# A streamed x + alpha * fx on one core: loads and stores interleaved, against all loads first and all stores last

## The chip, the core and the metric

The kernel runs on one core of a Trainium2 chip. The metric is the time of one execution on the device in microseconds (us); the median of three runs stands for a kernel. Beside it one profiled execution gives the trace that is read here. Its span goes from the first to the last instruction on the core and is a little shorter than the time of a run.

## What is computed

```python
B, S, D = 512, 32, 640
x, fx: bfloat16 [512, 32, 640]      # 20.97 MB each
alpha: bfloat16 [1]

def reference(x, fx, alpha):
    return x + alpha * fx
```

Two arrays are read, one of the same size is written, and each element is used once: 62.92 MB pass through the core.

## The kernel before

x, fx and out are seen as 128 partitions with one row each of 81,920 elements, which is 160 KiB in bf16. `K = 1024` elements, 2 KiB, is the unit in which the lists `X` and `FX` cut the row. x comes in three chunks (of 64, 64 and 32 KiB per partition) into a pool `wide` of two buffers; fx comes in five chunks (32, 32, 38, 32 and 26 KiB) into a pool `fs` of two buffers. `X_CUTS` splits the first chunk of x into transfers of 8 and 56 KiB, and `F_CUTS` splits the third of fx into 32 and 6 KiB.

`PLAN` is the order of the program, written out by hand, and it is all there is of loops: `x i` loads a chunk of x (`load_x`, L87), `f j` one of fx (`load_f`, L96), `a` loads alpha (L133) and spreads it over 128 partitions by a matmul of a row of ones (L135, L137) and a copy out of PSUM (L139), `c j i` computes where chunk j of fx and chunk i of x overlap (`compute`, L108), and `s i` stores a chunk (`store`, L121).

All transfers are issued by SyncE (SP) on one queue, in the order of the plan. SP waits, at an issue, for what that transfer needs, and everything behind it waits too. The computation is one instruction of VectorE for each piece, `scalar_tensor_tensor`, that multiplies fx by alpha and adds x in one pass, and writes over x. A store thus waits for the passes over its chunk. A load waits until the buffer is free: the third chunk of x for the end of the first store, later chunks of fx for the passes that read the earlier ones. One wait more is set by hand (`AFTER`): the first store is not issued before the first 32 KiB of the third chunk of fx have landed; the other 6 KiB are then still under way.

At the end SP waits for all transfers (a `nop`, L148).

Of the kernel before, what the change touches and what calls it, by code (L numbers as in the profile page):

```python
# [2 lines left out]

# [4 lines left out]

ACT = mybir.ActivationFunctionType
ALU = mybir.AluOpType  # L10
F32 = mybir.dt.float32
BF16 = mybir.dt.bfloat16

K = 1024
P = 128


X = [(0, 32), (32, 64), (64, 80)]
FX = [(0, 16), (16, 32), (32, 51), (51, 67), (67, 80)]

F_CUTS = {2: (48,)}
S_CUTS = {}
AFTER = {("s", 0): ("f", 2, 48)}
X_CUTS = {0: (4,)}
PLAN = """
x 0
a
f 0
f 1
x 1  # L30
c 0 0
f 2
c 1 0
s 0
f 3
x 2
c 2 1
f 4
c 3 1
c 3 2  # L40
s 1
c 4 2
s 2
"""


@with_exitstack
def kernel(
    ctx: ExitStack,
    tc: tile.TileContext,  # L50
    x: bass.AP,
    fx: bass.AP,
    alpha: bass.AP,
    out: bass.AP,
):

    nc = tc.nc
    xv = x.flatten_outer_dims().rearrange("(p n) d -> p (n d)", p=P)
    fxv = fx.flatten_outer_dims().rearrange("(p n) d -> p (n d)", p=P)
    ov = out.flatten_outer_dims().rearrange("(p n) d -> p (n d)", p=P)
    assert xv.shape[1] == X[-1][1] * K == FX[-1][1] * K

    consts = ctx.enter_context(tc.tile_pool(name="consts", bufs=1))
    psum = ctx.enter_context(tc.tile_pool(name="psum", bufs=1, space=bass.MemoryType.PSUM))
    wide = ctx.enter_context(tc.tile_pool(name="wide", bufs=2))
    fs = ctx.enter_context(tc.tile_pool(name="fs", bufs=2))  # L70
    ctx.enter_context(tc.manual_schedule())

    parts = {}
    info = mybir.DependencyInfo(mybir.DependencyClass.Sync, mybir.DependencyReason.DATA)

    def after(r, *what):
        if what in AFTER:
            tc.add_manual_dep(r.ins, parts[AFTER[what]].ins.name, info, reason="issue late")

    xt, ft = {}, {}  # L80
    done = []

    def load_x(i):
        a, b = X[i]
        xt[i] = wide.tile([P, max(e - s for s, e in X) * K], x.dtype, tag="x", name="x_t")
        for c, d in pairwise((a, *X_CUTS.get(i, ()), b)):
            r = nc.sync.dma_start(  # L87
                out=xt[i][:, (c - a) * K : (d - a) * K], in_=xv[:, c * K : d * K]
            )
            done.append(r)  # L90

    def load_f(j):
        a, b = FX[j]
        ft[j] = fs.tile([P, max(e - s for s, e in FX) * K], fx.dtype, tag="f", name="f_t")
        for c, d in pairwise((a, *F_CUTS.get(j, ()), b)):
            r = nc.sync.dma_start(  # L96
                out=ft[j][:, (c - a) * K : (d - a) * K],
                in_=fxv[:, c * K : d * K],
            )
            after(r, "f", j)  # L100
            done.append(r)
            parts["f", j, d] = r

    def compute(j, i):
        (fa, fb), (xa, xb) = FX[j], X[i]
        a, b = max(fa, xa), min(fb, xb)
        piece = xt[i][:, (a - xa) * K : (b - xa) * K]
        r = nc.vector.scalar_tensor_tensor(  # L108
            out=piece,
            in0=ft[j][:, (a - fa) * K : (b - fa) * K],  # L110
            scalar=lanes["a_f"][:],
            in1=piece,
            op0=ALU.mult,
            op1=ALU.add,
        )
        done.append(r)

    def store(i):
        a, b = X[i]
        for c, d in pairwise((a, *S_CUTS.get(i, ()), b)):  # L120
            r = nc.sync.dma_start(  # L121
                out=ov[:, c * K : d * K], in_=xt[i][:, (c - a) * K : (d - a) * K]
            )
            if c == a:
                after(r, "s", i)
            done.append(r)
            parts["s", i, d] = r

    lanes = {}

    def alpha_to_lanes():
        a_1 = consts.tile([1, 1], alpha.dtype, name="a_1")
        done.append(nc.sync.dma_start(out=a_1[:], in_=alpha[None, :]))  # L133
        ones = consts.tile([1, P], alpha.dtype, name="ones")
        nc.vector.memset(ones[:], 1.0)  # L135
        a_ps = psum.tile([P, 1], F32, name="a_ps")
        done.append(nc.tensor.matmul(a_ps[:], ones[:], a_1[:], start=True, stop=True))  # L137
        lanes["a_f"] = consts.tile([P, 1], F32, name="a_f")
        nc.vector.tensor_copy(out=lanes["a_f"][:], in_=a_ps[:])  # L139

    does = {"x": load_x, "f": load_f, "c": compute, "s": store, "a": alpha_to_lanes}
    for step in PLAN.split("\n"):
        if step:
            what, *of = step.split()
            does[what](*map(int, of))


    rest = nc.sync.nop(nofuse=True)  # L148
    for i in done[:-1]:
        tc.add_manual_dep(rest.ins, i.ins.name, info, reason="all but the last store")  # L150


# [1 line left out]
_INS = ['x', 'fx', 'alpha']  # L154
_OUTS = [((512, 32, 640), 'bfloat16')]


# [23 lines left out]
```

## Time and profile before

| | |
|---|---|
| median of 3 runs | 151.9 us (151.71 to 151.95) |
| span of the profiled execution (no other time is given for it) | 150.2 us |
| bytes read, written | 41.94 MB, 20.97 MB |
| mean rate over the span | 419 GB/s |

The page has a row for each engine (busy time and share of the span), for the DMA queue (packets, megabytes, share of the time of 16 DMA engines), and for groups of instructions: line, engine, operation, names and shapes, then busy time and mean duration, then the idle time before them and what ended it. Lines of the timeline and of the chain of waits begin with the start and the duration in us; SPq is SyncE issuing a transfer. Issue rows give the size and the time from issue to landing. A row of the view by windows has the stretch, its length, the busy time of four compute engines, the granted clock, the DMA share and GB/s; there a packet counts where it starts, so a window must be laid on the packets to be read.

### The profile page before, as it was taken

To read this page: it belongs to the slowest core of one execution; us is meant where nothing else is said; L and a number is where in the kernel's file an instruction comes from. 1 tells how busy PE (TensorE), PEld (TensorE's weight loads), DVE (VectorE), ACT (ScalarE), POOL (GpSimd) and SP (SyncE) were. 2 spreads that over 40 slices of the span, in tenths; PEclk is the share of its full clock that TensorE was granted. 3 is DMA by queue.
4 is the path that set the end of the run, shared out by engine and by line. 5 is a ranking of instruction groups with operands and counts; after the bars stand their busy time and mean duration, and the time that the engine had idled before them with its cause. 6 is when DMAs were issued, how large, how long until landed. Compare 5 with 4: busy or idle time off the path is not lost.

```text
span 150.2 us, 81 instructions
## 1 busy us (share of the span) xinstructions
PE 0.2 (0%) x1; PEld 0.1 (0%) x1; DVE 86.8 (58%) x8; POOL 0.2 (0%) x4
## 2 busy tenths in 40 slices
PE   0000000000000000000000000000000000000000
PEld 0000000000000000000000000000000000000000
DVE  0000000049999999970599998006999999980000
POOL 0000000000000000000000000000000000000000
DMA  5997999999999896999969696999999969697995
GB/s 179 589 412 321 489 384 419 419 445 436 515 419 489 349 559 279 419 419 397 650 279 559 279 559 279 419 419 419 428 469 418 570 279 559 279 559 314 428 436 218
DMA packets 1874, 62.92 MB, mean 419 GB/s; under 512 B 210, under 2 KB 210, under 8 KB 338
## 3 DMA queue, kind: packets, MB, share of 16 engines
q1 hardware_dynamic: 1874, 62.92, 98.1%
HBM read 41.94 MB, written 20.97 MB: 419 GB/s over the span
## 4 chain that ended last, share of the span: by engine, by line
DMA 53%; DVE 35%; SPq 1%; issue 0%; DVEq 0%
DMA f_t<-in_fx_dram 53%; DVE x_t L108 35%; SPq L87 1%; SPq L96 0%; SPq L133 0%; DVEq L108 0%
## 5 line engine op out<-in xcount | busy, mean ns | idle before, releaser
L108 DVE SCALAR_TENSOR_TENSOR x_t<-f_t,a_f,x_t 128x16384 bf16<-128x16384 bf16 (+3 forms) x6 | 86.5, 14438 | 25.5 <-DMA f_t<-in_fx_dram 25.5
L139 DVE COPY a_f<-a_ps 128x1 f32<-128x1 f32 x1 | 0.2, 157 | 21.4 <-PE a_ps L137 21.4
L135 DVE MEMSET ones<- 1x128 bf16 x1 | 0.2, 165 | 0.8 <-PEq L165 0.8
L137 PE MATMUL a_ps<-a,ones 1*128 1x1 bf16 x1 | 0.2, 159 | 22.2 <-DMA a<-in_alpha_dram 22.2
L165 POOL MEMSET const-bfloat16-1.0<- 128x1 bf16 x1 | 0.1, 103 | 0.0
L165 POOL MEMSET const-uint8-127<- 128x1 uint8 x1 | 0.1, 102 | 0.0
L137 PEld LDWEIGHTS <-ones 1*128 1x128 bf16 x1 | 0.1, 100 | 1.0 <-DVE ones L135 1.0
L165 POOL MEMSET const-float32-0.0<- 128x1 f32 x1 | 0.1, 100 | 0.2 <-issue 0.2
L165 POOL MEMSET const-float32-1.0<- 128x1 f32 x1 | 0.1, 99 | 0.0
## 6 DMA issues: line engine op xcount, KB each, us to landing
f_t<-in_fx_dram SPq DMA_DIRECT2D x4, 4096.0 KB, 30.6
x_t<-in_x_dram SPq DMA_DIRECT2D x1, 7168.0 KB, 21.2
x_t<-in_x_dram SPq DMA_DIRECT2D x1, 4096.0 KB
out_dram<-x_t SPq DMA_DIRECT2D x1, 4096.0 KB, 14.9
f_t<-in_fx_dram SPq DMA_DIRECT2D x1, 3328.0 KB, 26.9
x_t<-in_x_dram SPq DMA_DIRECT2D x1, 1024.0 KB, 4.6
f_t<-in_fx_dram SPq DMA_DIRECT2D x1, 768.0 KB, 23.0
out_dram<-x_t SPq DMA_DIRECT2D x2, 22.4
```

Source lines behind the costliest of these rows:

```text
L87: r = nc.sync.dma_start(out=xt[i][:, (c - a) * K : (d - a) * K], in_=xv[:, c * K : d * K])
L108: r = nc.vector.scalar_tensor_tensor(out=piece, in0=ft[j][:, (a - fa) * K : (b - fa) * K], scalar=lanes["a_f"][:], in1=piece, op0=ALU.mult ...
L135: nc.vector.memset(ones[:], 1.0)
L137: done.append(nc.tensor.matmul(a_ps[:], ones[:], a_1[:], start=True, stop=True))
L139: nc.vector.tensor_copy(out=lanes["a_f"][:], in_=a_ps[:])
L165: nc = _bacc.Bacc("TRN2", target_bir_lowering=False, num_devices=1)
```

## The change

The kernel's body is written anew. The unit `K` is now 512 elements, 1 KiB per partition. One flat tile `t` of 207.5 KiB per partition holds everything: x and the result lie at their own places, 0 to 160, and pieces of fx lie where there is room: beyond 160, and at places of x that is not loaded yet. `f a b p` loads fx from a to b to the place p; `place` finds it again.

The order: x from 0 to 64 (as 8 and 56 KiB), fx 0-64 (into the place of x 96-160), x 64-96, fx 64-111.5 (beyond 160). From there each load is issued when the passes over what lies in its place are done: x 96-114 after the add to 18, x 114-155 after the add to 64, fx 111.5-137.5 after the add to 88, fx 137.5-160 after the add to 111.5, x 155-160 after the add to 113.5. Only then come the stores, of 64, 64 and 32 KiB. The step `s 0 64 | f 137.5 160 184` carries a wait set by hand: the first store is issued when the last piece of fx has landed, and the 5 KiB of x 155-160 are the only load behind that piece on the queue.

The fused pass is replaced by two: `m`, `tensor_scalar_mul` of fx by alpha in place, rounded to bf16, and `c`, `tensor_add` of that to x in place. Alpha is loaded to eight partitions instead of one, right behind the first 8 KiB of x; the matmul reads one of them.

```diff
-K = 1024
 P = 128
+K = 512
+ROW = 160
+SPARE = 47.5
+
+LANES = 8
...
 PLAN = """
-x 0
+x 0 8
 a
-f 0
-f 1
-x 1
-c 0 0
-f 2
-c 1 0
-s 0
-f 3
-x 2
-c 2 1
-f 4
-c 3 1
-c 3 2
-s 1
-c 4 2
-s 2
+x 8 64
+f 0 64 96
+x 64 96
+f 64 111.5 160
+m 0 18
+c 0 18
+x 96 114
+m 18 64
+c 18 64
+x 114 155
+m 64 88
+c 64 88
+f 111.5 137.5 158
+m 88 111.5
+c 88 111.5
+f 137.5 160 184
+m 111.5 113.5
+c 111.5 113.5
+x 155 160
+s 0 64 | f 137.5 160 184
+m 113.5 137.5
+c 113.5 137.5
+m 137.5 160
+c 137.5 160
+s 64 128
+s 128 160
 """
...
-    wide = ctx.enter_context(tc.tile_pool(name="wide", bufs=2))
-    fs = ctx.enter_context(tc.tile_pool(name="fs", bufs=2))
+    flat = ctx.enter_context(tc.tile_pool(name="flat", bufs=1))
...
+    t = flat.tile([P, int((ROW + SPARE) * K)], x.dtype, name="t")
...
+    def place(a, b):
+        for c, d, p in reversed(lies):
+            if c <= a and b <= d:
+                return at(p + a - c, p + b - c)
...
+    def load_f(a, b, p):
+        lies.append((a, b, p))
+        done.append(nc.sync.dma_start(out=at(p, p + b - a), in_=of(fv, a, b)))
...
+        a_n = consts.tile([LANES, 1], alpha.dtype, name="a_n")
+        done.append(nc.sync.dma_start(out=a_n[:], in_=alpha[None, :].to_broadcast([LANES, 1])))
...
-        r = nc.vector.scalar_tensor_tensor(
-            out=piece,
-            in0=ft[j][:, (a - fa) * K : (b - fa) * K],
-            scalar=lanes["a_f"][:],
-            in1=piece,
-            op0=ALU.mult,
-            op1=ALU.add,
-        )
+    def multiply(a, b):
+        done.append(nc.vector.tensor_scalar_mul(place(a, b), place(a, b), lanes["a"][:]))
+
+    def add(a, b):
+        done.append(nc.vector.tensor_add(at(a, b), at(a, b), place(a, b)))
...
+        for other in later:
+            tc.add_manual_dep(done[-1].ins, begun[other].ins.name, info, reason="begins late")
```

More of the change, by code (lines that the diff above doesn't have):

```diff
@@ L1 @@
 from contextlib import ExitStack
-from itertools import pairwise
 import concourse.bass as bass
@@ L7 @@
 from concourse._compat import with_exitstack
-ACT = mybir.ActivationFunctionType
 ALU = mybir.AluOpType
 F32 = mybir.dt.float32
-BF16 = mybir.dt.bfloat16
-K = 1024
 P = 128
[L18 to L24, printed above, removed]
+K = 512
+ROW = 160
+SPARE = 47.5
+LANES = 8
 PLAN = """
-x 0
+x 0 8
 a
-f 0
-f 1
-x 1
-c 0 0
-f 2
-c 1 0
-s 0
-f 3
-x 2
-c 2 1
-f 4
-c 3 1
-c 3 2
-s 1
-c 4 2
-s 2
+x 8 64
[24 more added lines that the diff above has]
+s 128 160
 """
@@ L61 @@
     nc = tc.nc
[L62 to L65, printed above, removed]
+    xv, fv, ov = (
+        t.flatten_outer_dims().rearrange("(p n) d -> p (n d)", p=P) for t in (x, fx, out)
+    )
+    assert xv.shape[1] == ROW * K
     consts = ctx.enter_context(tc.tile_pool(name="consts", bufs=1))
@@ L68 @@
     psum = ctx.enter_context(tc.tile_pool(name="psum", bufs=1, space=bass.MemoryType.PSUM))
-    wide = ctx.enter_context(tc.tile_pool(name="wide", bufs=2))
-    fs = ctx.enter_context(tc.tile_pool(name="fs", bufs=2))
+    flat = ctx.enter_context(tc.tile_pool(name="flat", bufs=1))
     ctx.enter_context(tc.manual_schedule())
-    parts = {}
+    t = flat.tile([P, int((ROW + SPARE) * K)], x.dtype, name="t")
     info = mybir.DependencyInfo(mybir.DependencyClass.Sync, mybir.DependencyReason.DATA)
-    def after(r, *what):
-        if what in AFTER:
-            tc.add_manual_dep(r.ins, parts[AFTER[what]].ins.name, info, reason="issue late")
@@ L80 @@
-    xt, ft = {}, {}
+    lanes = {}
+    lies = []
     done = []
[L83 to L88, printed above, removed]
-            )
[L90 to L108, printed above, removed]
-            out=piece,
-            in0=ft[j][:, (a - fa) * K : (b - fa) * K],
-            scalar=lanes["a_f"][:],
-            in1=piece,
-            op0=ALU.mult,
-            op1=ALU.add,
[L115 to L133, printed above, removed]
+    def at(a, b):
+        return t[:, int(a * K) : int(b * K)]
+    def of(v, a, b):
+        return v[:, int(a * K) : int(b * K)]
+    def place(a, b):
+        for c, d, p in reversed(lies):
+            if c <= a and b <= d:
+                return at(p + a - c, p + b - c)
+        raise ValueError(f"fx {a} to {b} lies nowhere in one piece")
@@ L136, in alpha_to_lanes, with store @@
         a_ps = psum.tile([P, 1], F32, name="a_ps")
[L137 to L145, printed above, removed]
+        done.append(nc.tensor.matmul(a_ps[:], ones[:], a_n[0:1, :], start=True, stop=True))
+        lanes["a"] = consts.tile([P, 1], F32, name="a_f")
+        nc.vector.tensor_copy(out=lanes["a"][:], in_=a_ps[:])
+    def multiply(a, b):
+        done.append(nc.vector.tensor_scalar_mul(place(a, b), place(a, b), lanes["a"][:]))
+    def add(a, b):
+        done.append(nc.vector.tensor_add(at(a, b), at(a, b), place(a, b)))
+    def store(a, b):
+        done.append(nc.sync.dma_start(out=of(ov, a, b), in_=at(a, b)))
+    does = {"x": load_x, "f": load_f, "a": load_alpha, "m": multiply, "c": add, "s": store}
+    begun = {}
+    for step in filter(None, PLAN.split("\n")):
+        step, *later = step.split(" | ")
+        what, *numbers = step.split()
+        does[what](*map(float, numbers))
+        begun[step] = done[-1]
+        for other in later:
+            tc.add_manual_dep(done[-1].ins, begun[other].ins.name, info, reason="begins late")
     rest = nc.sync.nop(nofuse=True)
```

3 lines of the change are left out of this document (added).

## The prediction

> **What bounds the kernel now.** I read the page's totals first, to see which resource is full.
>
> ```profile
> span 150.2 us, 81 instructions
> PE 0.2 (0%) x1; PEld 0.1 (0%) x1; DVE 86.8 (58%) x8; POOL 0.2 (0%) x4
> q1 hardware_dynamic: 1874, 62.92, 98.1%
> ```
>
> One queue moves 62.92 MB, and its packets fill the 16 DMA engines for 98.1% of the span; VectorE works 58% of it. The DMA queue is the bound. A gain can only come out of what it loses now, and a loss comes from anything that leaves it empty.
>
> Next the chain of waits, the issues and the times to landing, to cut the span into stages of the queue. Sizes are in KiB per partition (1 KiB is 128 KiB in all, 512 elements); 480 of them pass, 320 in and 160 out.
>
> ```profile
> 0.73 0.38 SPq L87
> 1.16 0.42 SPq L87
> 1.99 30.13 DMA f_t<-in_fx_dram
> 49.92 22.95 DMA f_t<-in_fx_dram
> 93.51 26.93 DMA f_t<-in_fx_dram
> ```
> ```profile
> 2.96 0.45 SPq L87 DMA_DIRECT2D x_t<-in_x_dram  x1
> 71.09 0.35 SPq L121 DMA_DIRECT2D out_dram<-x_t  x1
> 71.48 0.43 SPq L96 DMA_DIRECT2D f_t<-in_fx_dram  x1
> 92.87 0.33 SPq L87 DMA_DIRECT2D x_t<-in_x_dram  x1
> 102.61 17.41 DVE L108 SCALAR_TENSOR_TENSOR x_t<-f_t,a_f,x_t 128x13312 bf16<-128x13312 bf16 x2 [9.13 <-DMA f_t<-in_fx_dram]
> 116.72 0.34 SPq L121 DMA_DIRECT2D out_dram<-x_t  x1
> 134.58 0.34 SPq L121 DMA_DIRECT2D out_dram<-x_t  x1
> ```
> ```profile
> x_t<-in_x_dram SPq DMA_DIRECT2D x1, 7168.0 KB, 21.2
> out_dram<-x_t SPq DMA_DIRECT2D x1, 4096.0 KB, 14.9
> x_t<-in_x_dram SPq DMA_DIRECT2D x1, 1024.0 KB, 4.6
> x_t<-in_x_dram SPq DMA_DIRECT2D x1, 58.3
> ```
>
> Landings follow: the first 8 KiB of x at 0.73 + 4.6 = 5.33; x to 64 at 1.16 + 21.2 = 22.36; f to 32 at 1.99 + 30.13 = 32.12; x from 64 to 128 at 2.96 + 58.3 = 61.26; f to 96 at 71.09, when the first store is issued on it; f to 102 at 72.87; store 0 at 92.87, when the load that needs its buffer is issued; f to 134 at 102.61; f to 160 at 120.44; the last store at 134.58 + 14.9 = 149.48. Time per KiB: 0.3041 for the 56 KiB of x, 0.3035 for the 96 KiB from 32.12 to 61.26, **0.3125 for store 0** (20.0 us for 64), 0.3044 for the load after it, **0.3074 for the 58 KiB that end at 120.44**, 0.3025 for the last 96 KiB, all stores. Loads alone and stores alone run alike; two stages at a change of direction run slower. Windows laid on the packets there:
>
> ```profile
> 70.30:72.30 2.00, 0.00 (x0) 0.00 (x0) 0.00 (x0) 0.00 (x0) 1.00 1.59 676
> 72.30:74.70 2.40, 0.00 (x0) 0.00 (x0) 1.70 (x1) 0.00 (x0) 1.00 1.01 437
> 86.50:88.90 2.40, 0.00 (x0) 0.00 (x0) 2.40 (x1) 0.00 (x0) 1.00 1.01 437
> 88.90:91.70 2.80, 0.00 (x0) 0.00 (x0) 2.80 (x1) 0.00 (x0) 1.00 1.05 374
> 117.20:119.60 2.40, 0.00 (x0) 0.00 (x0) 2.40 (x1) 0.00 (x0) 1.00 1.17 437
> ```
>
> The last two columns are the DMA share and GB/s; a window counts the packets that start in it. The byte rate over the share is the rate of a busy engine set: 437/1.01 = 433 GB/s in mid-stage. In 88.90 to 91.70, the last piece of store 0 with a load queued behind it, it is 374/1.05 = 356: 1.05 MB were busy for 2.94 us instead of 2.42, **0.52 us lost**. In 117.20 to 119.60, the last piece of f with store 1 behind it, 437/1.17 = 374: 2.81 instead of 2.42, **0.39 lost**. In 70.30 to 72.30, before store 0, 676/1.59 = 425: 3.18 instead of 3.12, 0.06 lost. The engines are busy in all three: these are slow packets, not an empty queue.
>
> **The change part by part.** *Order of the queue.* Bytes stay at 480 KiB per partition; 6 + 4 + 3 large transfers replace 4 + 6 + 3, so nothing is added there, and the first 8 KiB and the last 32 KiB are as before. Three changes of direction become one. Removed: the store-to-load one (0.52) and one of the load-to-store ones. The one left is issued when f has landed, with 5 KiB of x behind it, 5 x 0.3035 = 1.52 us. Its price lies between 0.06 and 0.39; I take 0.06, since its nearest row is store 0, issued 1.78 us ahead of the end of what was queued (71.09 to 72.87), and not store 1, issued some 3 us ahead. By this count the gain is 0.52 + 0.39 + 0.06 - 0.06 = 0.91. By stages: 5.33 + 312 x 0.3035 = 100.0 for the loads, + 160 x 0.3025 = 48.4 for the stores, + 0.06 = 148.5 against 149.48, a gain of 1.0; with all loads at 0.3041 to 0.3044, as three of the stages ran, 0.2 to 0.3 less. I take **0.8 us**, with 0.5 (only the store-to-load price goes) and 1.0 as its ends.
>
> *The start of the first store.* Does 1.52 us of cover suffice? The lead from issue to data: the first load is issued at 0.73, and
>
> ```profile
> 1.00:1.50 0.50, 0.00 (x0) 0.10 (x1) 0.00 (x0) 0.00 (x0) 1.00 0.00 0
> 1.50:2.00 0.50, 0.00 (x0) 0.00 (x0) 0.00 (x0) 0.00 (x0) 1.00 0.88 197
> ```
>
> so data start 0.8 to 1.3 later. With some 0.1 from landing to issue the store's data come at most 1.4 after the landing: covered, by 0.1 at least. If the cover did not count at all, 1.4 would be lost. The Trainium skill (DMA: Bandwidth & Descriptors, Anatomy of one DMA) gives a transfer a fixed cost near 2.0 us, most of it the receipt of the last byte, stated for another path of issue. By that the store would come about 0.5 late, for a time near 151.6; store 0 here, issued on a landing, followed without a gap after at most 1.78 us, so the trace puts the sum below 1.8 and cannot say more.
>
> *VectorE.* Each fused pass becomes a multiply in place and an add. Their rows:
>
> ```profile
> L108 DVE SCALAR_TENSOR_TENSOR x_t<-f_t,a_f,x_t 128x16384 bf16<-128x16384 bf16 x2 | 34.5, 17281 | 9.7 <-DMA f_t<-in_fx_dram 9.7
> L135 DVE MEMSET ones<- 1x128 bf16 x1 | 0.2, 165 | 0.8 <-PEq L165 0.8
> L139 DVE COPY a_f<-a_ps 128x1 f32<-128x1 f32 x1 | 0.2, 157 | 21.4 <-PE a_ps L137 21.4
> ```
>
> The fused pass takes 17281/16384 = 1.055 ns per element, 0.54 us per KiB. Neither new pass is in the trace. Upper end: each as dear as the fused one, 1.08 per KiB for the pair. Lower end: the memset's 128 elements take 8 ns more than the copy's one, 0.06 ns per element, 0.03 per KiB and pass. What can be afforded, p per KiB, comes from the queue's own times, because SP issues in order and a load now waits for the adds that free its place. f to 64 lands at 32.12 + 32 x 0.3035 = 41.8, and from there VectorE runs on. The queue holds loads up to 41.8 + 79.5 x 0.3035 = 66.0, then x 96-114 to 71.4, x 114-155 to 83.9, f 111.5-137.5 to 91.8, f 137.5-160 to 98.6, x 155-160 to 100.1. Each must be issued 1.3 before the one ahead of it ends. x 96-114: 18p by 64.7, p up to 1.27. **x 114-155**: 64p by 70.1, p up to 0.44. f 111.5-137.5: 88p by 82.6, 0.46. **f 137.5-160**: 111.5p by 90.5, 0.436. x 155-160 needs 2 KiB more once f 111.5-137.5 has landed at 91.8, under 2.2 us even at the upper end, against 97.3. After the last load the add to 137.5 is due for store 64-128 at 100.1 + 19.4 - 1.3 = 118.2, and the add to 160 for the last store at 137.5: 24p and 22.5p from 92 to 93 on, p up to 1.0. So the pair is free up to **p = 0.436** and then costs 111.5 us per unit of p: the 0.8 gain is used up at 0.443. Late loads make everything behind them late, since all stores stand last on the same queue. My value: priced by arithmetic operations, a fused pass holds two, so an add that reads the same two streams is half of it, 0.27; the multiply, with one operation and one stream, lies between 0.03 and 0.27. The middle is 0.42, inside the limit but narrowly. I take it as hidden at no cost. It is the weakest link: at 0.54 (both at half) 111.5 x 0.104 = 11.6 us are lost, and at 1.08 VectorE sets the end, 41.8 + 160 x 1.08 + 32 x 0.3025 = 224.
>
> The Trainium skill (VectorE: DVE Perf Modes, The perf-mode tier table) has 693 ns for 2048 bf16 elements of a multiply by a scalar, four per cycle, and 1224 ns for an add, two per cycle. An estimate from these is 0.40 per KiB with some 0.15 us per instruction, 46 us for the 111.5 KiB against 48.6 allowed, so the sum would stay as it is; no run here shows it yet.
>
> *Alpha* goes to eight partitions, from just behind the first transfer; one issue as before, and 41.8 us from its first use: nothing. Buffers: one flat tile replaces four, f lies where x comes later; its waits are the ones above.
>
> *Sum.* Span 150.2 - 0.8 = 149.4. The median of the runs shown is 151.9, 1.7 above the span, and that stays: **151.1 us**.
>
> **The rivals.** *A, the price stays.* The change to stores costs 0.39 wherever it is (0.33 more than in the sum) and the first store is some 0.25 late: the gain falls to 0.2, **151.7**. For it: store 1 lost 0.39 though it was issued early enough; against it: store 0 lost 0.06. *B, VectorE late (slower).* At x 114-155 or f 137.5-160, from p = 0.443 on; **152.5 at 0.449, 162.7 at 0.54**. For it: the only bf16 pass of this size costs 0.54 by itself, and the limit is close; against it: VectorE has 42% of the span idle now, and the pair needs only to cost less than four fifths of the fused pass, with one operation each. *C, all at the best rate.* No slow packets and every load at 0.3035 or better: 1.1 gained, **150.8**. For it: the last 96 KiB ran at 0.3025; against it: three load stages without a change ahead of them ran at 0.304. That the change does not do what it says is unlikely: SP issues in the program's order on one queue, and the store's wait is on a landing that the queue itself orders.
>
> **How the numbers follow.** Forecast 0.50 (151.1, its own range 150.8 to 151.4); A 0.21; B 0.17; C 0.12. Within 0.2%, or 0.3 us, of 151.9 no difference can be told. Faster than 151.6: the forecast, C and a small part of A, 0.64. Same: most of A and the edge of B, 0.18. Slower than 152.2: 0.18, B and a first store without cover (1.4 - 0.8 = 0.6 above 151.9). The range runs from 150.5, C with a little more, to 152.7, which takes in the lost cover and the mild cases of B.
>
> **What would show it.** Right: loads without a break to about 100, DMA windows near 433 GB/s per share throughout, the first store's data following the last x with no empty slice, the last landing near 148.7. For VectorE: a multiply and add of 46 KiB together below 20 us, and x 114-155 issued before 70. Wrong: a slice of the DMA row below 9 near 71 or 91 (B), or near 100 (A); if it gets slower with no empty slice, then a rate of packets that I took as fixed is not.

## The result and the profile after

| | before | changed |
|---|---|---|
| median of 22 runs, us | 151.92 | 151.41 |
| span of the profiled execution, us | 150.2 | 149.7 |
| forecast, us | | 151.1 (150.5 to 152.7) |

The changed kernel is faster: ratio 0.9962, 95% interval 0.9946 to 0.9977, which is 0.6 us (0.35 to 0.8); the medians and the two spans lie 0.5 apart. The forecast had the direction and put the gain at 0.8.

The totals of the changed kernel's page:

```profile
span 149.7 us, 91 instructions
PE 0.2 (0%) x1; PEld 0.1 (0%) x1; DVE 66.5 (44%) x16; POOL 0.2 (0%) x4
q1 hardware_dynamic: 1888, 62.92, 97.9%
```

The packets now take 0.979 x 149.7 = 146.6 us of each engine, against 0.981 x 150.2 = 147.3: some 0.8 us of packet time are gone, about what the forecast had. The span is only 0.5 shorter, so some 0.3 came back as time in which engines had nothing. The timeline and the chain of waits of the changed kernel say where (start, duration, engine and line, what):

```profile
78.24 13.53 DMA t<-in_fx_dram
81.51 6.43 DVE L118 TENSOR_TENSOR t<-t 128x12032 bf16<-128x12032 bf16 x1
87.96 0.33 SPq L102 DMA_DIRECT2D t<-in_fx_dram  x1
99.10 0.35 SPq L121 DMA_DIRECT2D out_dram<-t  x1
```

fx to 137.5 lands at 78.24 + 13.53 = 91.77, and fx to 160 just ahead of 99.10, when the first store is issued on it. These 22.5 KiB took 7.3 us, 0.325 per KiB against 0.3035 in the forecast: 0.5 us lost in one stage. Their load had been issued at 87.96, when the add to 111.5 was done, 3.8 us before the load ahead of it landed. Windows over that stage (stretch, length, busy time of four engines, granted clock, DMA share, GB/s):

```profile
89.00:91.00 2.00, 0.00 (x0) 0.00 (x0) 0.00 (x0) 0.00 (x0) 1.00 0.93 385
91.00:93.00 2.00, 0.00 (x0) 0.00 (x0) 1.17 (x3) 0.00 (x0) 1.00 0.99 403
93.00:97.00 4.00, 0.00 (x0) 0.00 (x0) 3.97 (x3) 0.00 (x0) 1.00 0.94 403
97.00:99.00 2.00, 0.00 (x0) 0.00 (x0) 2.00 (x1) 0.00 (x0) 1.00 0.89 373
```

Three of the four rows have a DMA share of 0.94 or less, and the rate over the share is 407 to 429 GB/s instead of 433: engines without work, and slow packets as well. How much that is can't be added up from windows, which cut packets; it is read from the landings, here and in the experiments. The stretch of the kernel before's last slow place, 117.20 to 119.60, is mid-store now, at the full rate:

```profile
117.20:119.60 2.40, 0.00 (x0) 0.00 (x0) 0.00 (x0) 0.00 (x0) 1.00 1.01 437
```

### The profile page after: what moved, and what is told of

It is laid out like the page before. It is cut to its first block, busy times and chain, and to the rows that moved or that the text cites. A ratio compares the mean times of both kernels' runs of the same rounds, so it can differ in the third digit from the quotient of the medians.

```text
span 149.7 us, 91 instructions
## 1 busy us (share of the span) xinstructions
PE 0.2 (0%) x1; PEld 0.1 (0%) x1; DVE 66.5 (44%) x16; POOL 0.2 (0%) x4
## 4 chain that ended last, share of the span: by engine, by line
DMA 36%; DVE 34%; issue 4%; SPq 1%; DVEq 0%
DMA t<-in_fx_dram 36%; DVE t L118 21%; DVE t L115 13%; SPq L98 0%; SPq L106 0%; DVEq L115 0%
## 5 line engine op out<-in xcount | busy, mean ns | idle before, releaser
L118 DVE TENSOR_TENSOR t<-t 128x12288 bf16<-128x12288 bf16 (+5 forms) x7 | 43.8, 6255 | 0.2
L115 DVE TENSOR_SCALAR t<-t,a_f 128x12288 bf16<-128x12288 bf16 (+5 forms) x7 | 22.8, 3264 | 40.0 <-DMA t<-in_fx_dram 40.0
## 6 DMA issues: line engine op xcount, KB each, us to landing
t<-in_x_dram SPq DMA_DIRECT2D x1, 5248.0 KB, 15.6
```

The source lines that it names most:

```text
L115: done.append(nc.vector.tensor_scalar_mul(place(a, b), place(a, b), lanes["a"][:]))
L118: done.append(nc.vector.tensor_add(at(a, b), at(a, b), place(a, b)))
```

## The experiments

Three groups of four kernels ran, each group on one chip beside the kernel before. On those chips the kernel before scattered more than in the first comparison (151.8 to 153.8 us), so kernels are compared within a group, and with their traces. Against it the changed kernel gained 0.6 us on one of these chips and 1.2 on another; why the kernel before scatters there was not found.

**The fused pass put back.** In the order of the changed kernel, `m` does nothing and `c` is the old pass:

```diff
-        done.append(nc.vector.tensor_scalar_mul(place(a, b), place(a, b), lanes["a"][:]))
+        pass
...
-        done.append(nc.vector.tensor_add(at(a, b), at(a, b), place(a, b)))
+        done.append(
+            nc.vector.scalar_tensor_tensor(
+                out=at(a, b),
+                in0=place(a, b),
+                scalar=lanes["a"][:],
+                in1=at(a, b),
+                op0=ALU.mult,
+                op1=ALU.add,
+            )
+        )
```

> The multiply and the add are put back into one fused pass of 0.54 us per KiB (1.055 ns per element), in the order of the changed kernel. Theory (from 0.436 us per KiB on, the loads are issued late and the queue runs empty): 111.5 x 0.104 = 11.6 us more, some 163.0, with empty slices near 72 and 100 us. Rival (VectorE is hidden anyway behind a queue that is full for 98% of the span): 151.4.

Measured 163.94 us (ratio 1.0713, 1.0676 to 1.075). Timeline and windows of that run:

```profile
76.48 0.33 SPq L98 DMA_DIRECT2D t<-in_x_dram  x1
```
```profile
71.00:77.40 6.40, 0.00 (x0) 0.00 (x0) 6.40 (x2) 0.00 (x0) 1.00 0.00 0
77.40:83.00 5.60, 0.00 (x0) 0.00 (x0) 5.60 (x1) 0.00 (x0) 1.00 1.12 435
100.00:104.00 4.00, 0.00 (x0) 0.00 (x0) 4.00 (x3) 0.00 (x0) 1.00 0.37 92
```

x 114-155 is issued at 76.48; from 71.0 to 77.4 not one packet starts while VectorE is busy throughout. So there is a limit for the pair of passes, as the prediction had it (one kernel beyond it does not tell where it lies), and the rival falls: in this order VectorE is hidden only because the two passes together are cheaper than the fused one. The other two rows show something more: after the gap the packets run at 435/1.12 = 388 GB/s instead of 433, and after a second gap, near 100 us, at 92/0.37 = 249 at first. A load that starts into an empty queue pays for its start twice here, with the lead of at least 0.9 us from issue to data and with slow first packets.

**The late wait of the first store, taken off or moved.** On one chip with the run above:

```diff
-s 0 64 | f 137.5 160 184
+s 0 64
```

> The wait set by hand is taken from the first store, so that it is issued right behind x 155-160, near 93.4 us, some 7 us before its turn. Theory (a store queued early slows the last piece of the load in front of it, as the last piece of f did before store 1 of the kernel before, 0.39 us): the slow packets come back at the change of direction, 151.6 to 151.9 us. Rival (the price of that piece has nothing to do with how early the store is queued): the engines that sat empty for some 0.3 us at the change are filled, 151.1 to 151.4.

Measured 152.24 (ratio 0.9965, 0.9937 to 0.9993), above what either theory had. In the other direction:

```diff
-s 0 64 | f 137.5 160 184
+s 0 64 | x 155 160
```

> The first store waits for the landing of x 155-160, the last load, instead of the last piece of fx; nothing is then under way when it is issued. Theory (the 5 KiB of x hide the lead from issue to data): the store's data come 0.9 us after an issue at some 100.7, against 99.95 to 100.3, so 1.2 us are added, 152.6. Rival (the cover counts for nothing, since the slowest engine sets the end): 151.4.

Measured 153.25 (ratio 1.0041, 1.0008 to 1.0073), 1.0 above the one without the wait. Timeline and windows of the kernel that waits for everything:

```profile
100.77 0.35 SPq L121 DMA_DIRECT2D out_dram<-t  x1
```
```profile
98.50:100.50 2.00, 0.00 (x0) 0.00 (x0) 2.00 (x1) 0.00 (x0) 1.00 0.62 256
100.50:101.50 1.00, 0.00 (x0) 0.00 (x0) 1.00 (x1) 0.00 (x0) 1.00 0.00 0
```

The store is issued 1.7 us later than in the changed kernel, and no packet starts between 100.5 and 101.5; the span of 151.4 is 1.2 to 1.7 longer than in the three traces of the changed kernel (149.7, 149.9 and 150.2), with 1.2 expected. So the 5 KiB of x do hide the lead of the store. What the run without the wait lost could not be told here, since the slow stage of fx was in it too; it is taken up again below.

**A store put back between the loads.**

```diff
 x 114 155
+s 0 64
...
 x 155 160
-s 0 64 | f 137.5 160 184
...
-s 64 128
-s 128 160
+s 64 111 | f 137.5 160 184
+s 111 160
```

> The store of 0-64 is put between the loads, right behind x 114-155, and the rest is stored as 64-111 and 111-160; three changes of direction instead of one, all else as in the changed kernel. Theory (each change has the price that the kernel before showed): 0.39 and 0.52 more, 152.3; if the store-to-load change alone counts, 151.9. Rival (the slow packets near 90 us come at a time, not at a change of direction, since the changed kernel shows some there too): no difference, 151.4.

Measured 152.08 (ratio 0.9947, 0.9924 to 0.997), with no changed kernel beside it; by the ratio it was no slower than the changed kernel had been elsewhere, which spoke for the rival. Hence both again, on one chip:

> The changed kernel unaltered, as the base for the three beside it on the same chip, and for a second trace of it. Both theories: 0.3% to 0.5% below the kernel before. The stretch near 91 us, where two engines lost 0.9 us each, tells whether such a loss is of that place (it comes again where f 137.5-160 begins) or of chance.

> The kernel with the store of 0-64 between the loads, on one chip with the changed kernel now. Theory (changes of direction have their price): 0.4 to 0.9 us above the changed kernel, with slow packets at the end of x 114-155, about 0.6, and at the end of the first store, about 0.5. Rival (only a store that is queued early slows the load ahead of it, and the way back to loads is free, as its first trace shows): 0.3 to 0.6 above. Second rival (nothing to do with direction): level with it.

The changed kernel came to 151.77 (0.9958, 0.9931 to 0.9985) and the one with the store between to 152.07 (0.998, 0.9956 to 1.0004): 0.3 apart, with runs that overlap. That is less than the theory had (0.4 to 0.9) and the lower end of what the first rival had (0.3 to 0.6). The second trace of the changed kernel loses again where f 137.5-160 comes: from the landing ahead of it to the first store it takes 7.45 us (91.79 to 99.24), as against 7.30 in the first trace (91.80 to 99.10). Windows of the kernel with the store between, on its two changes of direction:

```profile
79.50:81.90 2.40, 0.00 (x0) 0.00 (x0) 2.37 (x2) 0.00 (x0) 1.00 1.59 560
81.90:84.30 2.40, 0.00 (x0) 0.00 (x0) 2.40 (x1) 0.00 (x0) 1.00 1.01 437
98.00:100.90 2.90, 0.00 (x0) 0.00 (x0) 0.00 (x0) 0.00 (x0) 1.00 1.30 565
100.90:103.30 2.40, 0.00 (x0) 0.00 (x0) 0.00 (x0) 0.00 (x0) 1.00 0.67 291
103.30:107.00 3.70, 0.00 (x0) 0.00 (x0) 0.00 (x0) 0.00 (x0) 1.00 0.95 410
```

In the first row 1.34 MB are busy for 3.82 us instead of 3.10: 0.7 us lost at the end of the loads, in front of the store that had been queued since 68.7. The last three rows, the way back to loads, run at 565/1.30 = 435, 434 and 432: nothing lost, though it was there that the kernel before lost 0.52. So the excursion to a store and back has its price, 0.06 + 0.52 in the kernel before and 0.7 here, but which of its two ends pays is not what the forecast read from one trace. That the medians differ by 0.3 only has a reason: in this kernel f 137.5-160 is issued at 87.95, long before its turn, which now comes after the store, and its stage is not slow (6.86 us, 111.90 to 118.76).

**Two passes in the kernel before.**

```diff
-        r = nc.vector.scalar_tensor_tensor(
...
+        f = ft[j][:, (a - fa) * K : (b - fa) * K]
+        done.append(nc.vector.tensor_scalar_mul(f, f, lanes["a_f"][:]))
+        r = nc.vector.tensor_add(piece, piece, f)
```

> The kernel before with each fused pass replaced by a multiply in place and an add, nothing else. Theory (VectorE is off the path there, the gain comes from the order of the queue): within 0.2 us of the kernel before. Rival (slow packets at a change of direction need a VectorE pass beside them; here VectorE is idle at both, near 90 and 118 us): the 0.57 and 0.38 us of slow packets are gone and the time is 0.5 to 0.9 lower.

Measured 153.21 against 152.58 (ratio 1.0052, 1.0024 to 1.0081): slower by 0.6, which neither expected. VectorE is idle from 88.7 to 102.7 there, and the packets that start from 89.2 on still run at 76/0.22 = 345 GB/s, so the rival is out: slow packets come without a pass beside them, near 90 us and, in the last two rows, near 118. Timeline and windows of this run say what the faster passes did:

```profile
113.51 0.34 SPq L116 DMA_DIRECT2D out_dram<-x_t  x1
```
```profile
89.20:91.80 2.60, 0.00 (x0) 0.00 (x0) 0.00 (x0) 0.00 (x0) 1.00 0.22 76
117.40:118.30 0.90, 0.00 (x0) 0.00 (x0) 0.00 (x0) 0.00 (x0) 1.00 1.65 444
118.30:120.20 1.90, 0.00 (x0) 0.00 (x0) 0.00 (x0) 0.00 (x0) 1.00 0.74 224
```

Store 1 is issued at 113.51 instead of 116.72, because its passes are done earlier, and the last pieces of f in front of it run at 444/1.65 = 269 and 224/0.74 = 303 GB/s: 0.40 MB busy for 1.49 us instead of 0.92, and 0.43 MB for 1.41 instead of 0.98, 1.0 us in all where the kernel before lost 0.39. The difference, 0.6, is about what the kernel lost. A faster engine off the path made it slower, by queueing a store earlier; what an early store costs is tried by itself further down.

**A longer cover, and the late load of fx.** First the cover alone, on the chip of the last three:

```diff
-x 114 155
+x 114 150
...
-x 155 160
+x 150 160
```

> The last load of x is 150-160 instead of 155-160, so that 10 KiB, 3.0 us, are behind the last piece of fx when the first store is issued on it, and no engine is empty at the change. Theory (the slowest engine sets the end, and it is not empty in the changed kernel either; a store queued some 2 us ahead is not yet early): within 0.2 us of the changed kernel. Rival (the 0.35 us for which the mean engine is empty count): 0.3 less. Second rival (2 us ahead is early, as with store 1 of the kernel before): 0.3 to 0.4 more, with slow packets in x 150-160.

Measured 153.78 (ratio 1.0074, 1.0045 to 1.0102), 2.0 above the changed kernel, more than any theory had. Its timeline and windows, where the first store follows at 99.32:

```profile
88.02 0.33 SPq L102 DMA_DIRECT2D t<-in_fx_dram  x1
90.33 0.49 DVE L115 TENSOR_SCALAR t<-t,a_f 128x1024 bf16<-128x1024 bf16 x1 [2.34 <-DMA t<-in_fx_dram]
```
```profile
89.00:91.00 2.00, 0.00 (x0) 0.00 (x0) 0.63 (x2) 0.00 (x0) 1.00 0.70 242
91.00:93.00 2.00, 0.00 (x0) 0.00 (x0) 2.00 (x2) 0.00 (x0) 1.00 0.99 334
93.00:97.00 4.00, 0.00 (x0) 0.00 (x0) 3.97 (x2) 0.00 (x0) 1.00 0.95 392
97.00:99.00 2.00, 0.00 (x0) 0.00 (x0) 2.00 (x1) 0.00 (x0) 1.00 0.87 366
```

Most of the damage is ahead of the store: from the landing at 90.3 to its issue 9.0 us pass, against 7.45 in the changed kernel. (The other 0.6 or so lies in x 150-160, which lands at 103.0, 3.6 us behind that issue where 10 KiB take 3.0.) As 5 KiB of x went from the front to the end, the turn of f 137.5-160 came forward: the load ahead of that lands at 90.3 instead of 91.8, while its issue, tied to VectorE, stays at 88.0. Near 90 the engines are empty for 30% of the time, and behind that packets run at 334/0.99 = 337 GB/s. That gave a new theory for the 0.5 us that the changed kernel loses at the same place: its load of fx is late too, only less. In the last group it is issued in two parts, each some 7 us ahead of its turn:

```diff
-m 88 111.5
-c 88 111.5
-f 137.5 160 184
+m 88 100.5
+c 88 100.5
+f 137.5 150 184
+m 100.5 111.5
+c 100.5 111.5
+f 150 160 196.5
...
-s 0 64 | f 137.5 160 184
+s 0 64 | f 150 160 196.5
```

(The passes over 137.5-160 are cut at 150 as well.)

> The changed kernel unaltered, base for the three beside it on the same chip: 0.3% to 0.5% below the kernel before.

> The last piece of fx is loaded in two parts, 137.5-150 as soon as the adds have reached 100.5 (near 83.4 us) and 150-160 after the add to 111.5 (near 88.3), so that each is issued some 7 us ahead of its turn instead of 3; one transfer and four VectorE passes more. Theory (a load needs more than 3 us from issue to full rate on all engines; the 0.5 us that the stage of f 137.5-160 lost in two traces is that): no slow stage between 91 and 99, 0.3 to 0.5 below the changed kernel. Rival (the loss belongs to the stretch near 91 us, whatever is loaded there): level with it.

The changed kernel came to 151.51 (ratio 0.992, 0.989 to 0.995), the split one to 151.20 (0.9924, 0.9886 to 0.9962). The ratios are taken against scattered runs of the kernel before and cannot part the two; the medians are 0.3 apart, 9 of the 12 runs of the split one lie between 151.13 and 151.47, and 3 near 152.9, for which no reason was found. So the traces decide. The stage of f 137.5-160 begins with the landing on which the multiply of 128x1024 starts, and ends with the first store; first the changed kernel on this chip, then the split one:

```profile
92.00 0.49 DVE L115 TENSOR_SCALAR t<-t,a_f 128x1024 bf16<-128x1024 bf16 x1 [4.06 <-DMA t<-in_fx_dram]
99.58 0.35 SPq L121 DMA_DIRECT2D out_dram<-t  x1
```
```profile
91.86 0.49 DVE L120 TENSOR_SCALAR t<-t,a_f 128x1024 bf16<-128x1024 bf16 x1 [3.54 <-DMA t<-in_fx_dram]
98.78 0.35 SPq L126 DMA_DIRECT2D out_dram<-t  x1
```

The changed kernel takes 7.58 us there (7.30 and 7.45 in its other two traces), the split one 6.92, and 22.5 x 0.3035 is 6.83. Windows of the split one:

```profile
89.00:91.00 2.00, 0.00 (x0) 0.00 (x0) 0.00 (x0) 0.00 (x0) 1.00 0.94 405
91.00:93.00 2.00, 0.00 (x0) 0.00 (x0) 1.10 (x3) 0.00 (x0) 1.00 1.00 422
93.00:97.00 4.00, 0.00 (x0) 0.00 (x0) 3.97 (x3) 0.00 (x0) 1.00 1.00 422
97.00:99.00 2.00, 0.00 (x0) 0.00 (x0) 2.00 (x1) 0.00 (x0) 1.00 0.98 407
```

The loss that was looked for, 0.5 to 0.75 us, is down to 0.1. The span is 149.4, against 150.2 (149.7 and 149.9 elsewhere), and the stage accounts for most of that. The rival, a loss that belongs to the stretch near 91 us, falls: the same bytes pass there in full time. That it is the early issue and not the cut into two transfers is told by the kernel with the store between, where the uncut piece was issued well ahead of its turn, too, and took 6.86.

Beside it the cover and the wait were tried once more, now without the late load:

> As the split version, with x 150-160 as the last load, so that the first store is issued 3 us ahead of its turn instead of 1.5. Theory (the 2.0 us that a cover of 10 KiB lost before were the late load of fx, which is mended here; what is left is a store queued 3 us ahead, like store 1 of the kernel before): 0.1 to 0.4 above the split version. Rival (the longer cover itself costs 2 us): 1.5 to 2 above it. Second rival (an empty engine at the change costs, so the longer cover helps): 0.2 to 0.3 below.

(`x 114 150` and `x 150 160` in the split version.) Measured 151.22: level with the split version, below what the theory had. The longer cover costs nothing by itself; the second rival's gain, from filling the few tenths in which engines are empty at the change of direction, does not come either. The profiled run was one of the slower ones, 151.82, and shows where it lost its 0.6: x 114-150, issued at 68.46, took 14.6 us to land, where the same transfer, issued at 68.37 in the kernel with the longer cover alone, took 14.0 (the second row).

```profile
t<-in_x_dram SPq DMA_DIRECT2D x1, 4608.0 KB, 14.6
```
```profile
t<-in_x_dram SPq DMA_DIRECT2D x1, 4608.0 KB, 14.0
```

> As the split version, without the wait set by hand, so that the first store is queued some 6 us ahead. Theory (a store queued early slows the end of the loads ahead of it): 0.4 to 0.7 above the split version, with slow packets in the last 3 us of the loads and a wide spread of the engines at the end. Rival (what the version without the wait lost before came from the late load of fx): level with the split version.

(`s 0 64` without its wait in the split version.) Measured 151.55, all 7 runs between 151.42 and 151.77: 0.35 above the split version, a little less than expected. Issue and windows:

```profile
93.47 0.42 SPq L126 DMA_DIRECT2D out_dram<-t  x1
```
```profile
97.00:99.00 2.00, 0.00 (x0) 0.00 (x0) 2.00 (x1) 0.00 (x0) 1.00 1.00 358
```

The last loads ahead of the store run at 358 GB/s where the split version has 407/0.98 = 415. 0.72 MB are busy for 2.0 us instead of 1.65, which is 0.35 us lost; the split version loses 0.08 by the same count, so these two microseconds hold most of the difference.

## Why the prediction was right, and what it missed

*The bound* was right: the queue sets the end. Cheaper VectorE passes are of no use by themselves, as the two passes in the kernel before show (0.6 us slower).

*Changes of direction* were the right source, and the sum of their prices came near: 0.8 us of packet time went. Where each price sits was not read rightly. The kernel before paid 0.52 at its store-to-load change, the kernel with a store between the loads paid 0.7 at load-to-store and nothing on the way back. What holds in the traces shown is that a store queued 7 us or more before the loads ahead of it have landed slows the last of them (0.35 to 1.0 us), and that the stores issued on a landing with 1.5 to 1.8 us under way, before and after the change, did not. Between these it is open: store 1 of the kernel before was issued 3.7 us ahead (116.72 to 120.44, not the "some 3" of the prediction) and cost 0.39, and some 3 us cost nothing in the split version with the longer cover. Why the way back cost 0.52 in one kernel and nothing in the other stays open.

*The start of the first store* was right. From its issue at 99.10 to the end of the span pass 50.6 us, which is what the cover (1.5), the stores (48.4) and the end of the span behind the last landing (0.7, as before) add up to: nothing is lost there. Without the cover 1.2 to 1.7 us of span are lost, with 1.4 in the prediction.

*VectorE* was right, with 0.42 taken for the pair. Its passes over the first 111.5 KiB ran from 41.95 to 87.94, 46.0 us or 0.41 per KiB:

```profile
41.95 2.62 DVE L115 TENSOR_SCALAR t<-t,a_f 128x9216 bf16<-128x9216 bf16 x1 [36.18 <-DMA t<-in_fx_dram]
```

An estimate from the figures of the Trainium skill (VectorE: DVE Perf Modes, The perf-mode tier table) was 46 us; the trace agrees. The parts came out as well: the add takes 12.4 us for 46 KiB, 0.27 per KiB, as forecast, and the multiply 6.3 us, 0.14, near the 0.15 that the middle of its range gave:

```profile
L118 DVE TENSOR_TENSOR t<-t 128x23552 bf16<-128x23552 bf16 x1 | 12.4, 12426 | 0.0
L115 DVE TENSOR_SCALAR t<-t,a_f 128x23552 bf16<-128x23552 bf16 x1 | 6.3, 6349 | 0.0
```

The argument for the add, a price by arithmetic operations, is not shown by that: the multiply has one operation too and costs half of the add. Taking the middle for the multiply was luck in part, since its range reached to 0.27, and 0.54 for the pair would have been as late as the fused run.

The 11.6 us that the rival had for a pair at 0.54 were some 12.2 to 12.5 in the fused run, against 151.4 to 151.8 for the changed kernel elsewhere; the restarts of the queue with their slow first packets were not in its price.

*What failed is the lead of a load.* The forecast took 1.3 us from issue to data, from the first load, and so allowed f 137.5-160 to be issued until 90.5. It was issued at 87.96, and its stage still lost 0.5 us (0.6 and 0.75 in the other two traces). The term that put a late load at nothing up to p = 0.436 was mis-sized: VectorE stayed below that, at 0.41, and the load was late all the same. At this place an issue 3.8 us before the landing ahead of it cost 0.5 to 0.75, one 2.3 us before it 2.2 (the longer cover: 88.02 and 90.33; 9.0 us instead of 6.83), and one 7 us or more before it 0.1 (the split version). This took the gain from the 1.0 that the prediction counted by stages to the 0.5 measured. The prediction's 0.8 was a value taken between 0.5 and 1.0, with a price of a change, not a late load, as the reason for the lower end; that it came so near is luck in part. The result lies between the forecast and the 151.7 of rival A, but not by A's mechanism: the first store was neither late nor slow. The lead is not a general figure either. x 114-155 is issued some 3 us before the load ahead of it ends, and lands 15.6 us later, at 83.9, just when the forecast had it:

```profile
68.31 0.33 SPq L98 DMA_DIRECT2D t<-in_x_dram  x1
```
```profile
t<-in_x_dram SPq DMA_DIRECT2D x1, 5248.0 KB, 15.6
```

It was not always enough there: in the profiled run of the split version with the longer cover the same place lost 0.6, with the same lead. Nor does the price follow the lead alone: in the fused run f 111.5-137.5 was issued at 89.41, 1.9 us before x 114-155 landed (76.48 + 14.8), and landed 11.1 us later; its 26 KiB took 9.2 us instead of 7.9, a loss of 1.3, less than the 2.2 at a lead of 2.3.

```profile
t<-in_x_dram SPq DMA_DIRECT2D x1, 5248.0 KB, 14.8
t<-in_fx_dram SPq DMA_DIRECT2D x1, 3328.0 KB, 11.1
```

What sets the price of a late load was not found. The sign that the prediction named for it, a slice of the DMA row below 9 near 71, 91 or 100 us, can't be read: a slice counts packets where they start, and the row of the changed kernel has 6 and 7 in mid-store too, where the windows show the full rate.

```profile
DMA  5997996969999899979898989996997969696996
```

## What to carry to other kernels

Where one queue is the bound, look for the gain in its slow packets, and hold each transfer to a window of issue. Here a load was safe with 7 us of queue in front of it and not always with 3 to 4, and a store issued 1.5 to 3 us before its turn cost nothing in the changed order, one issued 7 us before it 0.35. Speeding up an engine that is off the path moves these issues, and can make the kernel slower. A change of the last transfers (here 5 KiB more cover) shifts the turn of everything ahead of them: check every issue that is tied to computing, not only the one that was meant.

## What the runs showed that was not expected

A full queue is not a full rate: the DMA share stays near 1 while packets in front of an early store run at 269 to 358 GB/s instead of 433, so only the rate over the share shows the loss. A load into an empty queue has slow first packets as well, 388 GB/s over the first 5.6 us of the first restart in the fused run. And a lead that is enough in one execution is not so in the next: the same transfer, issued within 0.1 us of the same time behind the same loads, took 0.6 us longer.
